# Moving vector work, two small products and a load order inside a fused gated spectral and feed-forward backward kernel

## Chip, cores and metric

The kernel runs on one core of one Trainium2 chip. The metric is the device time of one execution in microseconds (us). Executions of one kernel scatter (54 of the kernel before took 1246.7 to 1264.1 us), so a comparison uses the mean of several runs, taken in alternation with runs of the kernel before on the same chip. Every run listed here counted as fast, that is, undisturbed.

Five engines matter: PE (TensorE, matrix products), DVE (VectorE), ACT (ScalarE), POOL (GpSimd) and SP (whose queue issues most loads: 462 of the 567 in the kernel before). A timeline below lists one engine's instructions in order of time; the bracket behind one is how long the engine sat idle before it and what released it.

## The reference

The reference runs a forward function and its backward pass (cut to the core):

```python
x = A_x                                        # 2048 x 1024, bf16
g = sigmoid((x * gate_w).sum(-1, keepdims=True))
a = irfft2(rfft2(x) * (w_r + 1j * w_i))        # spectral filter
h = relu(B_x @ w1 + b1) ** 2                   # w1: 1024 x 3584
b = h @ w2 + b2                                # w2: 3584 x 1024
out = g * a + (1 - g) * b
# results: out, and the gradients of x, w_r, w_i, w1, b1, w2, b2, gate_w for a given grad_out
```

## The kernel before: the parts that matter

Big products are split into 2 x 2 quarters and done with seven block products (p1 to p7) in place of eight. This saves PE one product in eight and costs sums of quarters on VectorE (1.09 to 3.88 us each in the gradient of x): left sums S1 to S4 and right sums T1 to T4. p5 needs S1 and T1, p6 needs S2 and T2, p7 needs S3 and T3, p4 needs T4, and p3 needs S4. The VectorE order is the program's order (helper `dve` ties each instruction to the one before), except where a scheduler spreads the filter work among the rest.

The edges of the spectrum: copies first, then at once the product `sp` that reads them.

```python
def edges_through(ams, ed, low, mid):
    tied = lambda ins: after(ins, later["last"], mybir.DependencyClass.NoSync)
    tied(nc.vector.tensor_copy(out=ed[lanes[0], :, 1, :], in_=ed[lanes[0], :, 0, :]))
    # ... five more copies into ed (cut)
    sp = fps.tile([P, NM, 2, 4], FP32, name="sp", tag="ps2", bufs=2)
    # ... 32 small products sp <- ed x am (cut)
```

The filter's constant `ab` (the load of c_ab, 128 KB per step) has two buffers:

```python
mats[m] = fb.tile([P, 2, 2, P], FDT, name="ab", tag="ab", bufs=2)
ld(out=mats[m][:], in_=cten["ab"].ap()[:, m])
```

The gradient of w1 (the loop that ends with `b.p5()`, `b.p7()`) calls its left sums behind the last product's add: `left(g + 1, 3, 1, 2, tie=b.added)`.

The start of the gradient of x, where most of the change lies. `quarter` issues seven transposing loads, `load("d", 1)` the two loads of block x1, `put` finishes an output row block, `right` is a T sum:

```python
x0 = b
x0.p1()
right(T1, b12, q0)
a.p4()
load("d", 1)
for _ in quarter(b21, 1, 0):
    pass
right(T2, b22, T1)
put(2 * NB - 1)
a.p3()
put(2 * NB - 2)
x0.p5(True)
right(Bx["T3"], b22, b12)
x0.sums(4)
x0.p6()
# ... (cut: fetches)
x1 = Block("d", 1)
x1.sums(3, 1, third=third)
x1.p1(second)
x1.sums(2)
x1.p5(True)
x0.p7()
x1.p6()
x1.sums(4)
right(T4, b21, T2)
x0.p3()
```

The end: the gate's row product `prow` needs a transpose and a reduction on VectorE and comes ahead of the last two block products.

```python
pr = more.tile([P, H], FP32, name="prow", tag="pZ", bufs=2)
pe(mm(pr[0:32, 0:32], lhsT=part, rhs=sel[:], start=True, stop=True))
nc.vector.tensor_copy(out=row_, in_=pr[0:32, 0:32])
st(out=out_8.rearrange("(b c) -> b c", c=32), in_=row_)
a.done = lambda t: close_x(t, ld)
a.p4()
a.p3()
```

## Time and profile before

| | kernel before |
|---|---|
| median of 3 runs | 1254.84 us (1254.78 to 1256.40) |
| the profiled run | 1251.3 us, span 1249.5, mean granted PE clock 0.994 |
| PE busy, DVE busy | 1218.9 us (98%), 767.5 us (61%) |
| half clock within the work | 6.83 us from 288.6, 3.41 from 1070.3, 3.41 from 1080.5 |

PE is the bound, but not a bound that this change can lower. What matters is which waits of PE remain, and how the clock answers to them. The lines for this are in the prediction below. One more view belongs beside them: VectorE's timeline of the kernel before, where PE waits for S1 of x1 (written as odd<-odd). The columns are start, length, engine, line, operation, result<-operands and shapes.

```profile
1073.69 3.88 DVE L1256 TENSOR_TENSOR w1q<-w2L,w1q 128x7168 f16<-128x7168 bf16 x1
1077.50 1.09 DVE L1192 TENSOR_TENSOR dS<-even,dS 128x1792 f16<-128x1792 bf16 x1
...
1079.62 1.09 DVE L1192 TENSOR_TENSOR odd<-odd 128x1792 f16<-128x1792 bf16 x1
```

VectorE does not idle here: the 3.88 us sum T3, which only the product after p5 needs (p7), stands ahead of S1, which PE is waiting for. The cure is a different order.

### The profile page before, as it was taken

What the parts mean: (1) busy time and instruction counts of PE and PEld (TensorE: products, weight loads), DVE (VectorE), ACT (ScalarE), POOL (GpSimd) and SP (SyncE); (2) the same over time, 40 slices, a digit from 0 to 9 for tenths busy, and PEclk for the clock granted to TensorE, in tenths of its full rate; (3) what the DMA queues carried; (4) which work ended last, traced back from release to release, by engine and by line L of the source; (5) the groups of instructions that cost most, each with busy time, mean ns of one, the idle gap of its engine ahead of it and who ended that gap; (6) DMA issues with size and microseconds to landing.
All of it is one profiled execution on the core that took longest, in us unless ns stands there. A gap on an engine that the chain in (4) does not pass through costs nothing.

```text
span 1249.5 us, 18801 instructions
## 1 busy us (share of the span) xinstructions
PE 1218.9 (98%) x6656; PEld 589.3 (47%) x6656; DVE 767.5 (61%) x1734; ACT 622.1 (50%) x1128; POOL 373.1 (30%) x615
## 2 busy tenths in 40 slices
PE   9999999999999999999999999999999999899997
PEld 5555545544444443444444455555544444344443
DVE  3556456665888869667676435454466657676464
ACT  4657667744877853434345456656422233133332
POOL 0124424422555432323335656654100000000000
PEclk9999999998999999999999999999999999899999
DMA  9567475665678769889899899986893559646550
GB/s 291 187 194 188 139 194 173 186 172 118 196 175 222 197 166 207 173 185 230 219 191 265 176 264 235 208 194 173 224 247 107 173 156 226 186 143 189 148 151 34
DMA packets 332824, 234.35 MB, mean 188 GB/s; under 512 B 198220, under 2 KB 291562, under 8 KB 332730
## 3 DMA queue, kind: packets, MB, share of 16 engines
q1 hardware_dynamic: 301856, 142.50, 51.1%
q0 software_dynamic: 30672, 90.61, 22.7%
q8 instruction: 52, 0.85, 0.3%
q14 instruction: 42, 0.34, 0.1%
q10 hardware_dynamic: 202, 0.04, 0.0%
HBM read 107.24 MB, written 81.81 MB: 151 GB/s over the span
## 4 chain that ended last, share of the span: by engine, by line
PE 81%; DVE 6%; issue 2%; DMA 2%; ACT 1%; POOL 0%; DVEq 0%; POOLq 0%
PE pw L1028 15%; PE ph L724 12%; PE pX L1196 12%; PE pd L734 12%; PE pV L1196 9%; PE pX L900 6%; PE pV L900 4%; PE acc L1290 4%; PE pui L309 1%; DMA ab<-c_ab 1%; PE pu L309 1%; PE pki L562 1%; PE px L413 1%; PE pk L276 1%; PE pv L444 1%
## 5 line engine op out<-in xcount | busy, mean ns | idle before, releaser
L724 PE MATMUL ph<-xT,w1g 128*128 128x512 bf16 x896 | 220.4, 380 | 1.2 <-DMA w1g<-in_B_w_dram 1.2
L734 PE MATMUL pd<-dbT,w2T 128*128 128x512 bf16 x896 | 213.9, 381 | 0.0
L738 DVE SCALAR_TENSOR_TENSOR dhT<-pd,rT 128x512 bf16<-128x512 f32 x112 | 77.1, 688 | 103.7 <-PE pd L734 97.7
L734 PEld LDWEIGHTS <-w2T 128*128 128x128 bf16 x896 | 87.5, 98 | 103.2 <-issue 2.2
L1028 PEld LDWEIGHTS <-res 128*128 128x128 bf16 x896 | 86.1, 98 | 97.0
L724 PEld LDWEIGHTS <-w1g 128*128 128x128 bf16 x896 | 85.3, 98 | 93.6 <-DMA w1g<-in_B_w_dram 1.5
L1028 PE MATMUL pw<-odd,res 128*128 128x512 bf16 x512 | 115.1, 379 | 0.0
L726 ACT ACTIVATE rT<-ph,b1col 128x512 bf16<-128x512 f32 x112 | 77.1, 688 | 64.9 <-PE ph L724 64.7
L225 POOL DMA_DIRECT2D z_scr<-u x96 | 58.6, 616 | 107.5 <-ACT u L293 52.8
L1196 PEld LDWEIGHTS <-dS 128*128 128x128 f16 x574 | 56.4, 99 | 72.1 <-DVE wT L1256 2.9
L1028 PE MATMUL pw<-even,res 128*128 128x512 bf16 x384 | 86.3, 379 | 0.0
L416 ACT CAST x<-px 64x512 f16<-64x512 f32 x128 | 74.1, 579 | 19.1 <-PE px L413 18.0
L1030 ACT CAST wo<-pw 128x512 bf16<-128x512 f32 x56 | 32.6, 585 | 81.6 <-PE pw L1028 81.6
L727 ACT ACTIVATE h2T<-rT 128x512 bf16<-128x512 bf16 x112 | 70.5, 629 | 2.3
L225 POOL DMA_DIRECT2D r<-y_scr x96 | 58.3, 611 | 37.6 <-DMA r<-y_scr 15.8
L1196 PEld LDWEIGHTS <-odd 128*128 128x128 bf16 (+1 forms) x392 | 38.6, 99 | 50.5 <-DVE odd L1192 3.5
L1196 PEld LDWEIGHTS <-even 128*128 128x128 bf16 (+1 forms) x392 | 38.3, 98 | 50.4 <-DVE wT L1256 2.5
L1136 POOL DMA_DIRECT2D out_dram<-ot x16 | 8.6, 540 | 171.5 <-DVE ot L1135 159.6
L1217 DVE TENSOR_TENSOR cu<-pV,u 128x512 f16<-128x512 f32 x28 | 19.3, 691 | 56.7 <-PE pV L1196 39.3
L900 PEld LDWEIGHTS <-S 128*128 128x128 f16 x336 | 32.4, 98 | 45.4 <-DVE S L887 7.2
L1169 POOL DMA_DIRECT2D out_dram<-gxo x14 | 7.6, 540 | 149.8 <-DVE gxo L1168 149.8
L453 POOL DMA_DIRECT2D y_scr<-pc x64 | 35.8, 560 | 51.1 <-DVE pc L450 36.2
(244 smaller groups left out, 2269.2 us busy)
## 6 DMA issues: line engine op xcount, KB each, us to landing
h2T_scr<-h2T POOLq DMA_DIRECT2D x28, 512.0 KB, 4.6
dhT_scr<-dhT POOLq DMA_DIRECT2D x28, 512.0 KB, 5.4
z<-z_scr SPq DMA_DIRECT2D x64, 128.0 KB, 3.2
y_scr<-pc POOLq DMA_DIRECT2D x64, 128.0 KB, 4.2
ax_scr<-yo POOLq DMA_DIRECT2D x32, 256.0 KB, 5.2
w1g<-in_B_w_dram SPq DMA_DIRECT2D x14, 512.0 KB, 4.9
out_dram<-wo POOLq DMA_DIRECT2D x56, 128.0 KB, 5.7
even<-h2T_scr SPq DMA_DIRECT2D x8, 896.0 KB, 6.0
```

The lines of the kernel that those rows point to most:

```text
L225: issue(out=a, in_=b) if stored else issue(out=b, in_=a)
L416: nc.scalar.copy(out=x[lanes[n], c, :, 0:HW], in_=px[lanes[c], n])
L453: st(out=y_scr[:][c, :, :, h].rearrange("r x t l -> (r x) t l"), in_=pc[:, n])
L724: mm(ph[:], lhsT=w1g[:, dc, fc % 2 * P : (fc % 2 + 1) * P], rhs=xT[:, dc, ss], start=(dc == 0), stop=(dc == DC - 1))
L726: nc.scalar.activation(rT[:], ph[:], ACT.Relu, bias=b1col[:, fc : fc + 1])
L727: nc.scalar.activation(h2T, rT[:], ACT.Square)
L734: mm(pd[:], lhsT=w_[:, ec, fc % FGC * P : (fc % FGC + 1) * P], rhs=dbT[:, ec, ss], start=(ec == 0), stop=(ec == DC - 1),)
L738: return STT(out=dhT, in0=pd[:], scalar=2.0, in1=rT[:], op0=ALU.mult, op1=ALU.mult, accum_out=gb1part[:, fc, sb : sb + 1],)
L900: self.mm = mm(acc[:], lhsT=lhs[:, t, c_], rhs=rhs[:, t, :], start=start and t == 0, stop=t == KH - 1, skip_group_check=True,)
L1028: mm(pw[:], lhsT=xr[:, t, d_ * P : (d_ + 1) * P], rhs=cur[:, t, :], start=(t == 0), stop=(t == NT - 1))
L1196: pe(mm(acc[:], lhsT=lhs[:, c, :], rhs=rhs[:, c, :], start=start and c == 0, stop=c == KH - 1, skip_group_check=True,))
L1290: turn["PE"] = mm(acc[:], lhsT=blks["h", k][:, c, t2 * P : (t2 + 1) * P], rhs=w_[:, c, :], start=(c == 0), stop=(c == FC - 1))
```

## The change

The intent: give VectorE each sum in the order of its deadline, and put PE's small products where their operands are ready. Six places, lettered as in the prediction: A the edges, B the start of the gradient of w1, C its left sums, D the output blocks, E the gradient of x, F the gate's row. The core of the diff:

```diff
-        def edges_through(ams, ed, low, mid):
+        def edges_ready(ed, low, mid):                         # A: copies only
+        def edges_through(ams, ed):                            # A: product and results
-        ex = edges_through(*edge)
+        edges_ready(*edge[1:])
         for _ in filler:
             yield
+        ex = edges_through(*edge[:2])
...
-        return 0.0 if left_[0] < 5 else 1.6 if "mid" in later else 1.55
+        return 0.0 if left_[0] < 6 else 1.6 if "mid" in later else 1.55   # B
...
             a.p3()
+            if second and g + 1 < FG:                          # C
+                left(g + 1, 3, 1, tie=a.ended)
...
-                left(g + 1, 3, 1, 2, tie=b.added)
+                left(g + 1, 2, tie=b.added)
...
         b.sums(3, 1, 2)                                        # D: T3 behind p2's add
-        for _ in made:
-            pass
...
             b.p2()
+            if a is None:
+                for _ in made:
+                    pass
...
             b.p5()
             b.sums(4)
+            if last:
+                right(T1, q1, q0)                              # E: T1 ahead of the put
             if a is not None:
                 put(2 * k - 2)
...
+        x0, ends = b, []                                       # E
+        a.done = ends.append
+        x0.sums(3, 1)
         x0.p1()
-        right(T1, b12, q0)
         a.p4()
         load("d", 1)
         for _ in quarter(b21, 1, 0):
             pass
+        x0.sums(2)
         right(T2, b22, T1)
-        put(2 * NB - 1)
         a.p3()
-        put(2 * NB - 2)
+        x0.sums(4)
         x0.p5(True)
+        x1 = Block("d", 1)
+        x1.sums(3, 1, third=third)
+        x0.p6()
         right(Bx["T3"], b22, b12)
-        x0.sums(4)
-        x0.p6()
...
         x1.sums(2)
+        for t in ends:
+            close(t)
+            put(t)
         x1.p5(True)
...
-        x1.sums(4)
         right(T4, b21, T2)
         x0.p3()
+        x1.sums(4)
...
+        a.done = lambda t: close_x(t, ld)                      # F: row behind p4
+        a.p4()
         pr = more.tile([P, H], FP32, name="prow", tag="pZ", bufs=2)
...
-        a.done = lambda t: close_x(t, ld)
-        a.p4()
         a.p3()
```

## The prediction

> **What bounds the kernel now.** I read the page's busy shares first, then the list of what TensorE (PE) waited for, then TensorE's timeline round each wait, and last VectorE's (DVE) timeline in the same stretch. The shares:

> ```profile
> span 1249.5 us, 18801 instructions
> PE 1218.9 (98%) x6656; PEld 589.3 (47%) x6656; DVE 767.5 (61%) x1734; ACT 622.1 (50%) x1128; POOL 373.1 (30%) x615
> ```

> PE is busy 1218.9 of 1249.5 us. The change adds and removes no matmul and no VectorE work, so all it can win is in the 30.6 us without a matmul, and in matmuls that ran slow. The longest PE waits (microseconds in total, times, longest):

> ```profile
> PE pX L900 <- DVE S L887: 4.5, 3, 1.6
> PE pX L1196 <- DVE wT L1256: 4.3, 2, 2.4
> PE pV L1196 <- DVE odd L1192: 3.0, 1, 3.0
> PE prow L1425 <- DVE w2R L1421: 2.7, 1, 2.7
> PE sp L361 <- DVE ed L352: 2.3, 1, 2.3
> PE pV L1196 <- DVE cu L1217: 1.8, 1, 1.8
> PE px L413 <- DMA ab<-c_ab: 1.4, 1, 1.4
> PE pV L900 <- DVE even L887: 1.3, 1, 1.3
> ```

> Seven of these eight are PE waiting for VectorE, though VectorE is busy only 61%: it is not short of time, it does things in the wrong order. They sum to 19.9 us; the rest of the 30.6 is the start (three waits, 2.9), the drain after the last matmul (4.7), the c_ab load (1.4) and crumbs under 0.3. PE's timeline (start, length; waiting time in brackets) shows a second cost:

> ```profile
> 288.74 0.19 PE L361 MATMUL sp<-ed,am 128*128 128x4 f16 x2 [2.34 <-DVE ed L352]
> ...
> 290.80 3.62 PE L734 MATMUL pd<-dbT,w2T 128*128 128x512 bf16 x8
> ...
> 1069.84 4.88 PE L1196 MATMUL pX<-wT,dS 128*128 128x512 f16 x14 [2.37 <-DVE wT L1256]
> ...
> 1080.77 4.74 PE L1196 MATMUL pV<-wT,odd 128*128 128x512 f16 x14 [3.02 <-DVE odd L1192]
> ...
> 1099.56 3.19 PE L1196 MATMUL pX<-wT,even 128*128 128x512 f16 x14 [1.97 <-DVE wT L1256]
> ```

> Eight matmuls normally take 1.89 us here and fourteen 3.19; after three of the waits they took 3.62, 4.88 and 4.74. The clock records hold half speed for 6.83 us from 288.6 and for 3.41 us each from 1070.3 and 1080.5. So those waits cost 2.34+3.41, 2.37+1.69 and 3.02+1.55 us. The 1.97 and the 2.71 (for prow) had no such tail.

> [...] idle times of 2.34 to 3.02 us were enough here, and 2.71 once was not[...]. [...] the trace has 1.22 us for 128x2048 (S sums), and in proportion 1.09 for 128x1792 and 3.89 for 128x7168[...].

> **The change part by part.** Six places, each from its own stretch of the timelines.

> A, edges. The edge product sp stood in the first chain after its copies were programmed; PE came to it at 286.4 and the last copy it needed (ed, L352) ended at 288.7. Now the copies stay and the product goes behind the row product, which the built order puts four chains of 8 matmuls later: some 7 us, with the copies ready by 289. Saved: 2.34+3.41 = 5.75, less perhaps 0.3, because row product, edge product and px now follow each other on two PSUM buffers. I take 5.5.

> B, start of the gradient of w1. The pacing stops one unit earlier (6 for 5), so VectorE has no filter work left there. It ran 3.0 us of it (y and pc sums, 468.8 to 471.75) before the first big sum T1. Without it T1 starts at 468.8; T1, S3, one add and S1 took 5.1 us, so they are ready at 473.9, and PE needs them at 467.8 + 4 chains of 1.73 + px and pv of 0.43 = 475.6. T2 and S2 add 3.4, to 477.3, when PE comes at 477.3. Saved: 1.25+1.44 = 2.7, I take 2.5.

> C, left sums two products on. S3, S1, S2 (3 x 1.22 = 3.7 us) stood behind the add of the last product, and S2 came 1.58 us late at 551.70 and 1.52 at 604.20. With S3 and S1 done earlier, S2 is ready 2.4 us sooner. Their transposed loads land 10 us or more before the new place (e.g. 529.4 for a sum now near 541). Saved 3.1.

> D, output blocks. The 3.88 us sum T3 stood ahead of the add that frees the bank pV, and p5 waited 1.80 us at 943.42. Behind the add, it still ends (943.4) before p7 (944.5) needs it. Saved 1.8.

> E, gradient of x. Before: S and T1 (from 1059.9), one closing, T2 to 1069.8, closings, T3 to 1077.5, then x1's sums, then T4 to 1099.5: 2.37, 3.02 and 1.97 of waiting and 3.24 of half clock, 10.6 in all. After: T1 goes right behind the last p5 (1053.2 to 1057.1); S3 and S1 of x0 end at 1062.2, S2 at 1063.3, T2 at 1067.2, where PE arrives at 1067.3: first wait gone. x1's sums would follow at 1068.8, but its two loads are issued at 1062.6 and 1065.4 behind five transposes on the same queue; the first landed at 1070.4, and the second's packets (512 bytes) ran from 1069 to about 1073. So S1 ends near 1075.5 and p5, which PE would start at 1073.5, waits about 2 us. T3 follows 3.9 us on, while p5 takes 3.0: 0.8. Then S2, two closings (2 x 2.9) and the add of p7 stand before x0.p3 may write its bank: about 7.5 against PE's two chains of 3.0: 1.5. T4 (3.9) ends before p2 and p3 (6.0) do: its wait is gone. Left: about 4.3. Saved: 6.3; half clock after the 2 us wait, at a third, costs 1.7: I take 5.7.

> F, the gate's row. prow waited 2.71 us for the reduction ending at 1238.4. Behind p4 (3.02 us) it finds it ready. A little is lost as p3's bank is freed by an add ending about 0.2 later. Saved 2.4; the 4.7 us after the last matmul stay.

> Sum: 5.5+2.5+3.1+1.8+5.7+2.4 = 21.0 us. As all of it is PE's own idle or slow time, it is on the path one for one.

> **The rivals.** First: the loads become the bound in E, and PE pays the half clock again. For it: those issue times, and DMA engines near fully occupied from 1064 to 1077. Whole, with 3 us of wait and the tail, E saves 4 and the time is near 1236. Second: VectorE's changed order gives new waits elsewhere. The scheduler moves the filter work through the whole gradient of w1; p6 of the third block had 2.9 us of slack and keeps about 1; the c_ab wait may move. For it: PE has no slack at 98%; against: VectorE is at 61%. It would cost 1 to 5 us: 1234 to 1238. Third: everything closes. Then 25 to 27 us go and the time is 1228 to 1230, just at 2%. Against: the loads in E. Fourth: nothing is gained, because loads bound the stages anyway. Against: PE waited for a load only 1.4 us after the start.

> **Range and chances.** The profiled run took 1251.3 us, the timed ones 1254.8: 3.5 us more, about two half-clock windows of 1.7, which I read (not shown) as longer tails behind the same waits. Without the waits part goes too; I add 1.3. 1254.84 - 21.0 - 1.3 = 1232.5. All but C and D carry 1 to 2 us of doubt, and the scheduler 3: 1228 to 1238. Two per cent is 1229.7, which needs 25 us: 0.2. Slower would need new waits of 47 us: 0.01.

> **What would show it.** Right: PE's busy time falls some 5 us through less half clock; waits for ed, w2R L1421, S in the loop and cu at the output blocks are gone from the list; at the gradient of x the first PE wait is for S1 of x1 (odd), 1 to 3 us, whose own releaser is a load of odd, then smaller ones for w1q and cu; no wait for T4. Wrong: a wait over 2 us in the gradient of w1, half clock at new places, prow or p3 waiting at the end, or no wait at x1's p5, which would mean the loads came earlier than I read.

## The result

The changed kernel is correct. Its median is 1234.58 us over 4 runs (1232.72 to 1237.12); the kernel before in the same set has 1254.81 (4 runs). The ratio is 0.9845, with a 95% interval of 0.9815 to 0.9874: within 2% of the kernel before. A ratio here is the mean time of one kernel's fast runs over that of the other's of the same rounds, so it is not quite the ratio of the quoted medians.

The first fence is the changed kernel's busy line; the one after it is from another profiled run of the same kernel (run `again` below). The first trace lacks 121 of 6656 matmul records, the second has all:

```profile
PE 1205.8 (98%) x6535; PEld 588.1 (48%) x6656; DVE 766.3 (62%) x1734; ACT 622.6 (50%) x1128; POOL 374.9 (30%) x615
```

```profile
PE 1213.8 (98%) x6656; PEld 588.4 (48%) x6656; DVE 765.5 (62%) x1734; ACT 622.9 (50%) x1128; POOL 374.4 (30%) x615
```

The complete trace shows PE busy 5.1 us less than before (1218.9): the same matmuls, less of them at half clock. What PE waited for in the changed kernel (us in all, times, longest):

```profile
PE px L415 <- DMA ab<-c_ab: 3.8, 1, 3.8
PE pX L1201 <- ACT u L1211: 1.5, 2, 0.9
PE pki L565 <- DVE rf L557: 1.4, 1, 1.4
PE pV L1201 <- DVE odd L1197: 1.2, 1, 1.2
...
PE pw L1033 <- DMA odd<-dhT_scr: 0.9, 1, 0.9
PE pV L1201 <- DVE cu L1222: 0.7, 1, 0.7
PE pb L851 <- DVE gb1b L849: 0.7, 1, 0.7
PE pX L1201 <- DVE w1q L1261: 0.6, 1, 0.6
```

Five of the eight entries of the old list are gone: S and even in the gradient of w1, wT, ed at the edges, and w2R (for prow). The longest is now a load, and ACT's copies u, which the old list lacks, stand second. PE's timeline shows the edges behind the row product without a wait, and the start of the gradient of x at full clock, 3.19 us for every chain of fourteen:

```profile
292.15 0.25 PE L1561 MATMUL prow<-sel,even 128*32 128x32 f32 x2
292.33 0.56 PE L363 MATMUL sp<-ed,am 128*128 128x4 f16 x16
...
679.27 0.60 PE L415 MATMUL px<-pm,ab 128*128 128x512 f16 x2 [3.75 <-DMA ab<-c_ab]
...
1051.04 3.18 PE L1201 MATMUL pX<-wT,odd 128*128 128x512 f16 x14 [0.87 <-ACT u L1211]
...
1067.54 3.19 PE L1201 MATMUL pV<-wT,odd 128*128 128x512 f16 x14 [1.23 <-DVE odd L1197]
1071.34 3.19 PE L1201 MATMUL pX<-w1q,dS 128*128 128x512 f16 x14 [0.61 <-DVE w1q L1261]
...
1078.27 3.18 PE L1201 MATMUL pV<-w2L,dS 128*128 128x512 bf16 x13 [0.72 <-DVE cu L1222]
```

(A chain shown as x13 lacks a record.) VectorE's timeline of the same stretch has the reason for the 1.23: S1 itself waited for a load.

```profile
1066.39 1.09 DVE L1197 TENSOR_TENSOR odd<-odd 128x1792 f16<-128x1792 bf16 x1 [3.43 <-DMA odd<-dhT_scr]
```

The two profiled spans differ by 1249.5 - 1233.6 = 15.9 us. They add up by part (before to after; "half" is half the length of the half-clock windows or what a chain took too long):

| part | predicted | in the two profiles |
|---|---|---|
| A edges | 5.5 | wait 2.34 and half clock 3.41 gone: 5.75 |
| B start of gradient of w1 | 2.5 | waits 1.25 + 1.44 gone, one of 0.71 (pb) new: 1.98 |
| C left sums | 3.1 | 1.58 + 1.52 gone: 3.10 |
| D output blocks | 1.8 | 1.80 gone |
| E gradient of x | 5.7 | 10.60 became 0.87 + 1.23 + 0.61 + 0.72 = 3.43: 7.17 |
| F gate's row | 2.4 | 2.71 became 0.67, and the end after the last matmul 6.01 for 4.71: 0.74 |
| elsewhere | none | c_ab 3.75 for 1.44, odd 0.85, rf 1.40 new: minus 4.56 |
| sum | 21.0 | 15.98 |

The timed medians of this set differ by more, 20.2 us, and the first and the third set of experiments gave 22.5 and 24.9. The last column is one pair of runs; the experiments say what of it is stable.

### The profile page after: what moved, and what is told of

The parts are those of the page before. It is cut to its first block, busy times and chain, and to the rows that moved or that the text cites. A ratio compares the mean times of both kernels' runs of the same rounds, so it can differ in the third digit from the quotient of the medians.

```text
span 1233.6 us, 18682 instructions
## 1 busy us (share of the span) xinstructions
PE 1205.8 (98%) x6535; PEld 588.1 (48%) x6656; DVE 766.3 (62%) x1734; ACT 622.6 (50%) x1128; POOL 374.9 (30%) x615
## 4 chain that ended last, share of the span: by engine, by line
PE 79%; DMA 5%; DVE 4%; issue 2%; ACT 2%; SPq 0%; POOL 0%; DVEq 0%; POOLq 0%
PE ph L727 13%; PE pd L737 12%; PE pX L1201 12%; PE pw L1033 12%; PE pV L1201 9%; PE pX L903 6%; PE pV L903 5%; PE acc L1295 4%; PE pu L309 1%; PE pui L309 1%; PE pk L276 1%; PE pki L565 1%; PE px L415 1%; PE pv L446 1%; DMA ab<-c_ab 1%
## 5 line engine op out<-in xcount | busy, mean ns | idle before, releaser
L727 PE MATMUL ph<-xT,w1g 128*128 128x512 bf16 x869 | 215.2, 379 | 2.9 <-DMA w1g<-in_B_w_dram 1.2
L737 PE MATMUL pd<-dbT,w2T 128*128 128x512 bf16 x872 | 209.7, 379 | 1.1
L1033 PE MATMUL pw<-odd,res 128*128 128x512 bf16 x496 | 112.6, 379 | 1.7 <-DMA odd<-dhT_scr 0.9
L591 DVE TENSOR_TENSOR yo<-tt 128x512 f16<-128x512 f16 x32 | 13.6, 425 | 59.9 <-DMA ax_scr<-yo 59.5
L782 POOL DMA_DIRECT2D h2T_scr<-h2T x28 | 20.8, 742 | 98.4 <-ACT h2T L730 84.0
```

What stands on the lines that cost most here:

```text
L727: mm(ph[:], lhsT=w1g[:, dc, fc % 2 * P : (fc % 2 + 1) * P], rhs=xT[:, dc, ss], start=(dc == 0), stop=(dc == DC - 1))
L737: mm(pd[:], lhsT=w_[:, ec, fc % FGC * P : (fc % FGC + 1) * P], rhs=dbT[:, ec, ss], start=(ec == 0), stop=(ec == DC - 1),)
L1033: mm(pw[:], lhsT=xr[:, t, d_ * P : (d_ + 1) * P], rhs=cur[:, t, :], start=(t == 0), stop=(t == NT - 1))
```

## The experiments

Twelve experiments ran in three sets, each with 5 rounds on one chip. The kernel before had medians of 1253.83 (54 runs), 1253.97 (11) and 1253.46 (11). Theory: each part closes a wait of its own, part by part as in the table, and the new waits have causes of their own that can be removed. Main rivals: half clock rather than waiting is what the edges cost; new waits are the old ones given back; or loads are the real bound.

### First set: parts alone, on the kernel before

**again**: the changed kernel, unaltered.

> The changed kernel once more, beside the others on one chip. If the first result holds, 19 to 21 us below the kernel before (ratio 0.983 to 0.986), no wait on VectorE over 1.5 us, and the wait of px for the c_ab load again between 2 and 4 us. If that load wait was chance, it is at or below the 1.4 us of the kernel before.

Measured: 1231.29 us (1228.30 to 1237.44, 6 runs), ratio 0.9806 [0.9771, 0.9840]. The profiled run is the slowest of the six; it has a c_ab wait of 3.19 us with half clock behind it (3.41 us from 680.1), then 1.92 for odd, 1.45 and 1.05 for rf. The waits of the old list stayed away, x1's p5 did not wait at all, and 0.87, 0.41 and 0.71 were left in E.

**edges_only**: part A alone on the kernel before.

```diff
-        ex = edges_through(*edge)
+        edges_ready(*edge[1:])
         for _ in filler:
             yield
+        ex = edges_through(*edge[:2])
```

> The kernel before with the edge product alone moved behind the row product. My theory (a wait of 2.34 us plus half clock that costs 3.41 us): the wait for ed and the half clock at 289 us are gone and the time falls by 5 to 6 us (ratio about 0.9955). Rival (the slow matmuls after the wait have another cause): the time falls by 2 to 2.5 us and slow chains stay near 290 us.

Measured: 1249.01 us (22 runs), ratio 0.9969 [0.9949, 0.9989], which is 3.9 us. In the profile the wait and the half clock at 289 are gone, and the start of the gradient of w1 stands at 471.62 against 476.97, 5.35 us earlier. So part A does what was predicted where it stands. Part of it is not seen in the time. PE's timeline of this run shows where it can go, first at x1's p5, then at p4 behind the row product `prow`:

```profile
1075.13 5.36 PE L1199 MATMUL pV<-wT,odd 128*128 128x512 f16 x14 [4.70 <-DVE odd L1195]
...
1233.65 4.62 PE L1199 MATMUL pX<-wT,odd 128*128 128x512 f16 x14
```

The wait is 4.70 us here, against 3.02 before, because the chains ahead of it ran at full clock: PE came 1.69 us sooner relative to VectorE and waited 1.68 longer. The end was set by VectorE both times. Then p5 itself ran slow for 5.36 - 3.19 = 2.17 us. But all this nearly cancels: the chain after p5 starts at 1080.33, still 5.0 us sooner than before (1085.34). More is lost at the end. `prow` waits 2.71 us in both traces, but only here does half clock follow (3.41 us from 1233.2), which costs p4 4.62 - 3.19 = 1.43 us. The span is 3.5 us shorter.

**warm_sp**: the kernel before with 46 dummy products ahead of `sp`, which keep PE busy in most of the wait for the copies. Their result is overwritten.

```diff
+            for _ in range(46):
+                mm(sp[:].rearrange("p m n e -> p (m n e)"), lhsT=identb[:], rhs=identb[:], start=True, stop=True, skip_group_check=True)
```

> The kernel before with 46 dummy matmuls (128x128 by 128 columns, overwritten afterwards) put ahead of the edge product, so that TensorE is busy while it would wait; all else in place. If idle time is what halves the clock: no half clock near 289 us, the dummies take about 2.9 us in place of the 2.34 us wait, and the time falls by about 2.9 us although work was added. Rival (the chains are slow for lack of data or banks): the two chains stay at 3.6 and 2.5 us and the time rises by about 0.6 us.

Measured: 1258.48 us (1250.39 to 1268.53, 22 runs), ratio 1.0026 [1.0003, 1.0050]. Its trace at the edges:

```profile
285.00 2.73 PE L359 MATMUL sp<-identb 128*128 128x128 bf16 x46
...
288.52 0.75 PE L363 MATMUL sp<-ed,am 128*128 128x4 f16 x15 [0.79 <-DVE ed L352]
...
291.26 1.89 PE L736 MATMUL pd<-dbT,w2T 128*128 128x512 bf16 x8
```

With the idle time filled there was no half clock: eight matmuls took 1.89 us right behind it, not 3.62, and the gradient of w1 began 1.85 us sooner than before (475.12). So in the trace the half clock was the wait's doing. The time is a miss: it got longer by 0.26%, not shorter, and the profiled run (1252.9 us) is among its quicker ones. In that trace the 1.85 us were lost again to a wait of 1.69 us for rf at 763 us, which the trace before lacks, and to half clock behind `prow` (4.54 us for p4). Why the timed runs are slower is not settled: their mean clock (0.9931) equals that of the kernel before, so their 4.0 us more in the mean are not half clock.

**gradx_only**: part E alone on the kernel before (the E lines of the diff).

> The kernel before with VectorE's new order at the start of the gradient of x alone (T1 after the last p5, sums first, closings later). My theory: the waits of 2.37, 3.02 and 1.97 us and the half clock after two of them (10.6 us in all) become four waits of 0.6 to 1.3 us (3.4 us), so the time falls by about 7 us (ratio 0.994). Rival (the loads of odd hold it all the same): a wait of 3 us or more at p5 of x1 with half clock, and 3 to 4 us gained.

Measured: 1244.30 us (17 runs), ratio 0.9925 [0.9902, 0.9947], 9.4 us of 1253.8. The waits of E in its trace (PE's timeline):

```profile
1061.44 3.18 PE L1196 MATMUL pX<-wT,odd 128*128 128x512 f16 x14 [0.87 <-ACT u L1206]
...
1080.25 3.19 PE L1196 MATMUL pX<-w1q,dS 128*128 128x512 f16 x14 [0.52 <-DVE w1q L1256]
...
1087.17 3.18 PE L1196 MATMUL pV<-w2L,dS 128*128 128x512 bf16 x14 [0.71 <-DVE cu L1217]
```

They sum to 2.10 us against 10.60 before: 8.5 us at this place, 9.4 in the time. The span of the profiled run (1246.74 us, slower than the median) is only 4.7 us shorter, as this trace has other losses that the one before lacks: 1.97 us of waits for rf, rt and e, 0.75 more for c_ab, and half clock behind `prow` (4.88 us for p4). E is the largest part and alone is worth at least half as much again as the 5.7 us I had put on it.

### Second set: single mends on the changed kernel

The changed kernel itself did not run in this set, so what a mend gains over it in time was not measured. The four ratios to the kernel before, 0.9802 to 0.9828, cannot be told from those of the changed kernel in the other two sets, 0.9806 and 0.9802. What follows is read from the traces.

**ab_ahead**: the c_ab load one step earlier, with a third buffer. Every trace with that load in its old place has a wait for c_ab, of varying size: 0.98 to 2.19 us in the four on the kernel before, 0.69 to 3.75 in the eight on the changed one. So that the change lengthened this wait is not shown.

```diff
-            mats[m] = fb.tile([P, 2, 2, P], FDT, name="ab", tag="ab", bufs=2)
-            ld(out=mats[m][:], in_=cten["ab"].ap()[:, m])
+        def turns_of(m):
+            if m < NM:
+                mats[m] = fb.tile([P, 2, 2, P], FDT, name="ab", tag="ab", bufs=3)
+                ld(out=mats[m][:], in_=cten["ab"].ap()[:, m])
...
                     wn[m + 1] = filters(m + 1)
+                    turns_of(m + 2)
```

> The changed kernel with the c_ab matrices loaded one step further ahead in three buffers for two. Theory: the load waits for its buffer until 668 us and then stands behind 3.5 MB of w2L, so issued 13 us or more sooner it lands in time: the wait of px for c_ab (3.75 us) goes and the time is 2.5 to 4 us under the changed kernel. Rival: the stretch is bound by the queue itself, and another load (z, odd or w2L) takes over the wait, so nothing is gained.

Measured: 1230.83 us (6 runs), ratio 0.9828 [0.9803, 0.9853]. The list of loads (result<-source, count, size, us from issue to landing), first of the changed kernel from 660 to 684 us, then of this one from 640 to 684:

```profile
ab<-c_ab SPq DMA_DIRECT2D x1, 128.0 KB, 10.4
```

```profile
ab<-c_ab SPq DMA_DIRECT2D x1, 128.0 KB, 2.3
```

In the changed kernel the load stands on its queue behind seven weight loads of 512 KB (issued from 648.1 to 663.6 us, 12.5 us in the median until they landed), since its buffer comes free only then: pv, the last product before it that reads an `ab`, starts at 668.2, and the load is issued at 668.8. That it took 10.4 us because it waited its turn is my reading, not shown by itself. One step earlier it took 2.3, and the waits for c_ab, odd and rf are all gone from the trace. (For odd and rf this shows little: they are absent from again2 too.) But a wait of 2.71 us for the second S and T sums appeared at 473.7, with 3.41 us of half clock behind it, which eats the gain (see best3).

**loads_first**: x1's two loads ahead of the seven transposes on the SP queue.

```diff
-        for _ in quarter(b21, 1, 0):
+        for _ in quarter(b21, 1, 0, later["load"]):     # each transpose ordered behind x1's loads
```

> The changed kernel with the two loads of x1's block ahead of the seven transposes of b21 on the queue. Theory (the loads bound the start of the gradient of x in the changed kernel): the waits of 1.23 us (x1.p5 for odd), 0.61 (for w1q) and 0.72 (for cu) go, about 2.5 us gained on the changed kernel, and no wait for T4 comes in their place. Rival (VectorE itself is the bound there): VectorE's idle time before S3 and S1 goes but the later two waits stay, under 1.3 us gained.

Measured: 1228.89 us (6 runs), ratio 0.9802 [0.9779, 0.9825]. All waits at x1's p5, x0's p7 and x0's p3 are gone; PE's timeline:

```profile
1063.45 3.19 PE L1201 MATMUL pV<-wT,odd 128*128 128x512 f16 x14
1066.47 3.19 PE L1201 MATMUL pX<-w1q,dS 128*128 128x512 f16 x14
```

The eight traces of the changed kernel with the old load order all have the waits for w1q (0.2 to 0.6 us) and cu (0.7), and three of them have the one for odd (1.2 to 1.9); loads_first and best3, with the new order, have none of the three. So the load order is the cause of the first two, as the first rival of the prediction held, at a smaller size. For odd, which comes and goes, VectorE's line above (S1 waits 3.43 us for its load) points the same way, but two traces without it show little.

**put_first**: the put ahead of T1 again.

```diff
-            if last:
-                right(T1, q1, q0)
             if a is not None:
                 put(2 * k - 2)
+            if last:
+                right(T1, q1, q0)
```

> The changed kernel with the put of the output rows ahead of the 3.9 us sum T1 instead of behind it. Theory: the put frees the buffer that ScalarE's scaling of the next row waits for, and ScalarE's copy of u3 stands behind that, so the wait of p4 for u3 (0.87 us at 1051 us) goes and ScalarE's idle time of 4.7 us before na falls under 1.5 us; up to 0.9 us gained. Rival: T1 comes 0.6 us later and x0.p6 waits for T2 by as much; nothing gained.

Measured: 1229.21 us (4 runs), ratio 0.9805 [0.9780, 0.9829]. The 0.87 us wait for ACT is gone (PE's timeline):

```profile
1046.40 3.19 PE L1201 MATMUL pX<-wT,odd 128*128 128x512 f16 x14
```

In the changed kernel T1 (3.88 us) stands before the put that frees a row buffer. ACT's scaling `na` needs that buffer and waited 4.71 us for it, and ACT's copy u3, which p4 needs, stood behind the scaling. So a vector sum delayed PE by way of a third engine.

**last_swap**: p7 ahead of p5 in the last block, to have u3 ready for the last p4.

```diff
+            if last:
+                b.p7_mm()
             b.p5()
             b.sums(4)
...
-            b.p7()
+            b.p7_add() if last else b.p7()
```

> The changed kernel with p7 ahead of p5 in the last block, so that ScalarE's copy between p7 and p4 of the one bank is covered by p5. Theory: the wait of 0.67 us before the last p4 goes and nothing comes in its place: 0.5 to 0.7 us gained. Rival: p7 now waits for ScalarE's copy u2 or for S3, and nothing is gained.

Measured: 1231.61 us (4 runs), ratio 0.9822 [0.9798, 0.9845]. The 0.67 us wait is gone, but the row product waits again (PE's timeline):

```profile
1220.58 0.25 PE L1446 MATMUL prow<-sel,w2R 128*32 128x32 f32 x2 [3.07 <-DVE w2R L1440]
1221.17 4.87 PE L1201 MATMUL pV<-w2L,dS 128*128 128x512 bf16 x13 [0.35 <-DVE cu L1222]
```

The reduction's chain of VectorE work ended about 9 us after p5 began in both kernels. In the changed kernel three chains (p5, p7, p4) cover it; here p7 had gone ahead, two chains cover only 6 us, and PE waits for the rest and then runs at half clock. The miss shows what part F depends on.

### Third set: two parts undone, and three mends together

**again2**: the changed kernel on this set's chip.

> The changed kernel once more, unaltered, as the yardstick for the other three of this call on the same chip. All theories: 1228 to 1237 us, 0.980 to 0.985 of the kernel before. In its profile: a wait of px for the load of c_ab near 679 us (0.7 to 3.8), pb near 486 (0.7), pX for wT and odd near 1051 (0.9), p4 at the end for u (0.7), and at the gradient of x one wait of p5 for odd (1 to 2) or waits for w1q and cu of 0.6 to 0.7.

Measured: 1228.53 us (1227.96 to 1233.14, 6 runs), ratio 0.9802 [0.9774, 0.9830]. Its slowest run is again the profiled one, with a c_ab wait of 3.71 us and half clock behind it.

**no_pace**: part B undone.

```diff
-        return 0.0 if left_[0] < 6 else 1.6 if "mid" in later else 1.55
+        return 0.0 if left_[0] < 5 else 1.6 if "mid" in later else 1.55
```

> The changed kernel with one part undone: the pacing of the filter work again stops five units before the end, not six. My theory (B is worth about 2 us): T1, S1, T2 and S2 are late again at the start of the gradient of w1, with waits of 1.2 and 1.4 us near 472 and 475, the pb wait of 0.7 after them gone, and the time 1.5 to 2.5 us above the changed kernel. Rival (the edge part already shifted the stage so far that the pacing does nothing): the two waits do not come back and the time is the same within 0.7 us. A side question: whether the pacing has to do with the c_ab wait near 679; I expect not: it stays between 0.7 and 3.8 us.

Measured: 1231.59 us (6 runs), ratio 0.9823 [0.9792, 0.9854], 3.1 us over the changed kernel by the medians and 2.6 by the means, though the intervals overlap. The two waits are back in PE's timeline, to the hundredth:

```profile
471.59 1.90 PE L903 MATMUL pV<-T,even 128*128 128x512 f16 x8 [1.25 <-DVE even L890]
474.93 1.90 PE L903 MATMUL pX<-T,S 128*128 128x512 f16 x8 [1.44 <-DVE S L890]
```

The 0.7 us wait of pb is gone. It is thus part of what B costs, and B is worth 1.25 + 1.44 - 0.7 = 2.0 us in the trace.

**no_left**: part C undone.

```diff
-            if second and g + 1 < FG:
-                left(g + 1, 3, 1, tie=a.ended)
...
-                left(g + 1, 2, tie=b.added)
+                left(g + 1, 3, 1, 2, tie=b.added)
```

> The changed kernel with one part undone: the three left sums stand again together behind the add of the last product. My theory (C is worth 3.1 us): the two waits of pX for S of about 1.5 us each come back near 545 and 598, and the time is 2 to 3.5 us above the changed kernel. Rival (what stands still there lets the transfers behind it land in time, as the new waits for c_ab, odd and rf suggest): the two waits come back, but the c_ab, odd and rf waits near 679 to 800 shrink by about as much, and the time is within 1 us of the changed kernel.

Measured: 1237.20 us (1233.74 to 1239.76, 6 runs), ratio 0.9860 [0.9831, 0.9889], 8.7 us over the changed kernel by the medians and 7.3 by the means. PE's timeline has three waits for S, 4.5 us in all:

```profile
517.42 1.90 PE L903 MATMUL pX<-T,S 128*128 128x512 f16 x8 [1.54 <-DVE S L890]
...
571.01 1.90 PE L903 MATMUL pX<-T,S 128*128 128x512 f16 x8 [1.75 <-DVE S L890]
...
622.70 1.90 PE L903 MATMUL pX<-T,S 128*128 128x512 f16 x8 [1.23 <-DVE S L890]
```

These are not the two waits that part C removed, though I expected those near 545 and 598. The sums feed groups of blocks that read the buffers `even` and `odd` in turn. In all four traces of kernels without part C's edit and on the kernel before, the two waits stand in groups of `odd` (551.70 and 604.20 in the kernel before), and the groups of `even` wait 0.1 us at most. Here it is the other way round: the three groups of `even` wait, and those of `odd` (542.76 and 596.05) do not. Where a wait falls seems to go with how the filter's products px and pv and their sums are mixed in. At 571.01 and 622.70 none of them stands between the group's first product and the one that waits; in the same group as the third, the kernel before has pv there (at 627.52) and no wait. That the other parts of the change shifted this mix was not tested.

The mean granted clock of the timed runs is also lower (0.9978 against 0.9992), which by an estimate, 0.0014 x 1230, is 1.7 us more. So leaving C out costs more in this kernel than the 3.1 us I had said. The waits for c_ab (1.0 us), odd (1.1) and rf (none) are smaller than in the changed kernel's first profile, as the rival asks, but they are as small in no_pace (0.7, none, none), which has part C, and the time does not fall for it. So the rival, that the new waits are these given back, is not supported.

**best3**: ab_ahead, loads_first and put_first together.

> Three of the single edits together on the changed kernel: the c_ab load one step ahead with a third buffer, x1's two loads ahead of the transposes of b21, the put ahead of T1. My theory (the three waits are independent): no wait for c_ab, odd or rf near 679 to 800, none for u near 1051, none over 0.3 us at the gradient of x; left are pb (0.6), the last p4 (0.7), the start and the end: profile 1225 to 1228, timed 3 to 6 us below the changed kernel, 0.976 to 0.979 of the kernel before. Rival (some other load or VectorE sum is the next bound just behind): one or more new waits over 0.7 us show up and the gain is below 2 us.

Measured: 1229.70 us (1228.06 to 1231.94, 6 runs), ratio 0.9807 [0.9780, 0.9834]. Its profile has the shortest span of all, 1226.3 us, and every wait that the three mends were for is gone. The timed runs are no faster than the changed kernel's (1228.53), where 3 to 6 us were expected. VectorE's timeline and then PE's at the start of the gradient of w1:

```profile
471.35 2.29 DVE L873 TENSOR_TENSOR T<-dbn,T 128x4096 f16<-128x4096 bf16 x1 [2.90 <-DMA h2T_scr<-h2T]
473.56 1.22 DVE L896 TENSOR_TENSOR S<-even 128x2048 f16<-128x2048 f16 x1
```

```profile
474.83 1.90 PE L909 MATMUL pX<-T,S 128*128 128x512 f16 x8 [2.77 <-ACT vc L454]
```

PE's own line names ACT as the releaser, but that work was long done; VectorE shows it. T2 waited 2.90 us for the store of h2T, and the S2 that follows it was what PE needed. In this kernel the store landed 8.7 us after its issue, in the changed kernel 5.8, in time for T2. The same store takes 8.7 us in ab_ahead, where the same wait is 2.8. Both have the third `ab` buffer and the earlier loads, and loads_first and put_first have neither the edit nor the wait. So the edit brought the wait with it (the store takes 8.7 us in these two traces, 5.1 to 6.1 in the other eight of the changed kernel); whether the earlier load slows the store, or the new places in memory do, was not tried. A version with loads_first and put_first only would be the next to try; it has not run.

## Why the prediction was right, and where it was not

The medians of 1234.58, 1231.29 and 1228.53 us all lie in the range of 1228 to 1238, round the 1232.5 predicted. The mechanism, PE waiting for VectorE work in the wrong order, is shown by the parts done alone (A, E) or undone (B, C); D and F were not tried by themselves. Two of the signs of being wrong that it named did show: no wait at x1's p5, in two of the three profiles of the unaltered changed kernel, and half clock at a new place, behind c_ab near 680, in two. Two slips of its working change nothing: by its own sum, the first rival's E of 4 us gives 1234.2, not 1236; and 3.89 us for 128x7168 is what the trace has, while in proportion to 1.22 it would be 4.3.

## What to carry to other kernels

When the bound engine is at 98%, list its waits, and for each look at what the awaited engine did just before: a long piece of work with a later deadline is a cause that a change of order can mend. After a reorder, look for engines and queues one step away (ACT behind a buffer that VectorE frees, a load behind others on its queue), because most of the waits that appeared here are theirs. And do not size such a change from one pair of profiles: here the pair said 16 us and the timed runs 20 to 25, in part because the same wait can have half clock behind it in one run and not in the next.
